# Start of a windowed-attention and gated-FFN kernel: first loads on other queues, an edge mask on ScalarE, a decode in PSUM, and 600 steps in a written order

## Chip, cores and metric

One core of one Trainium2 chip. The time is device microseconds (us) of one execution of the program. The kernel before took 701.21 us, the median of 3 runs (701.18, 701.21 and 704.1).

## What is computed

The inputs are `x` of shape (4, 4160, 192) and `weight_gen` of shape (4, 4160, 8, 7), and the float32 weights of a feed-forward stage: `w_in` (192 x 1024), `conv_w` (3 x 1024) and `w_out` (1024 x 192).

```python
# stage 1: every position is a softmax-weighted sum of itself and the 6 positions before it, per head
w = exp(weight_gen - max(weight_gen, -1)); w = w / (sum(w, -1) + 1e-9)
x_pad = concatenate([zeros((B, 6, D)), x], axis=1)
x = einsum('bshk,bskhg->bshg', w, x_pad windows of 7).reshape(B, S, D)
# stage 2: gated feed-forward with a 3-tap convolution along the sequence
h = maximum(x @ w_in, 0)
conv = sum over k of conv_w[k] * h shifted by k - 1
out = (h * 1/(1 + exp(-conv))) @ w_out
```

## The kernel before

**Tiles.** The 4 x 4160 positions are cut into 128 segments of 130, one per partition. A block is 4 rows of each segment, 512 positions in all, and there are 33 blocks. The text calls them block 0, 1, 2 and so on.

**Attention of a block** (`head`). `w` is a tile of softmax weights: w0 serves block 0, w1 blocks 1 and 2, w2 blocks 3 and 4, w3 blocks 5 and 6. `ring` holds rows of x. Seven products `ring * w` (`tap`, L299, 128x768 each) go into `px` (four) and `py` (three), on POOL ("G") or VectorE ("V") as `PLAN` says. For blocks 0 to 2 TensorE transposes and adds all seven pieces itself (L347). From block 3 on, two DMAs that add while they copy (`fold1` L322, `fold2` L325) and a POOL addition (`fold3` L332) leave one piece for TensorE to transpose. The result is split into a rounded part H (ScalarE, L367) and a remainder (VectorE, L371).

**Feed-forward of a block.** A unit is one 128-column slice of w_in: five matmuls into a PSUM bank z (`mm1` L385), relu, middle tap and tanh on ScalarE (L391, L395, L409), two side taps and the gate on VectorE (L402, L447). Eight units make a block. `mm2` (L468) then multiplies by w_out, one 128-position output tile at a time.

**Weights.** The float inputs are read as raw bits and decoded in five steps (`decode_steps`, L140 to L158), then w_in is split into a high part (ScalarE, L663) and a low part (VectorE, L668). w_in comes in five pieces (`CH`): "m" pieces hold its first 128 rows, "f" pieces the other 64 rows, folded, which SyncE's queue then spreads (L682). f0 and m0 are columns 0 to 255, f1 and m1 256 to 511, m2 512 to 1023. `r_cw` is the raw `conv_w`; it is decoded in SBUF in a corner of `h` (24 partitions).

**Softmax of a `w` tile** (`sm_ops`). Maximum, subtraction, exp (ScalarE), sum, epsilon, reciprocal, normalization (L271). For the first 6 rows of each batch, `zero` (L276) multiplies by a 0/1 tile `edge`, since those rows look back before the sequence starts.

**What sets the order.** Every step is a task with an engine, a duration and dependencies. A list planner (`greedy`, `place`) places all tasks by estimated arrival times (`w_in_t`, `x_t_`, `CH`) and the program issues them in that order; each engine works in its own issue order. Steps of class "VK" are VectorE steps that read or write SBUF only. Ahead of the first POOL step after a VK step, a pair of tiny writes, `tok` (L960 on VectorE, L961 on POOL), makes POOL wait until VectorE has got there. The loads at the start are issued in program order on SyncE's and ScalarE's queues.

## Time and profile before

| | value |
|---|---|
| profiled execution | 701.24 us |
| its span | 699.5 us (1.74 us lie around it) |
| median of 3 runs | 701.21 us |
| busy: PE / DVE / ACT / POOL | 97% / 94% / 85% / 81% of the span |
| granted TensorE clock, mean | 0.995 |

PE is TensorE, DVE is VectorE, ACT is ScalarE, SP is SyncE, PEld the weight loads of TensorE. Busy shares are averages over the whole span: the start, where the change lies, has to be read from windows and the timeline. In a wait, the name behind the arrow is what ended it.

### The profile page before, as it was taken

Reading aid. Unit: us, or ns where it says so; the run is one execution under the profiler, and the core shown is the slowest. Engines: PE = TensorE matmul, PEld = TensorE weight load, DVE = VectorE, ACT = ScalarE, POOL = GpSimd, SP = SyncE. Lnnn points to the kernel's source line nnn. Section 1 sums busy time; section 2 is a strip of 40 time slices with the busy share of each in tenths; the row PEclk is TensorE's granted clock in tenths of the full one; section 3 lists DMA queues with packets and bytes.
Section 4 is the critical chain, followed back from the end, with each engine's and each line's share of the span. In section 5 each row is a group of like instructions: output and inputs, shape, how many; then the busy total and the mean of one; then the engine's idle time right before and its main releaser. Section 6 shows DMA issues by size and latency. Waiting matters only on the chain.

```text
span 699.5 us, 11223 instructions
## 1 busy us (share of the span) xinstructions
PE 676.5 (97%) x3749; PEld 615.3 (88%) x3749; DVE 657.0 (94%) x1067; ACT 597.3 (85%) x1140; POOL 568.8 (81%) x453
## 2 busy tenths in 40 slices
PE   1799999999999999999999999999999999999998
PEld 1688889999999999999999999999999999999998
DVE  6899999999999999999999999999999999999991
ACT  2488888988989998989899898989999898888982
POOL 3898899989899997989798898979799897981111
PEclk9899999999999999999999999999999999999999
DMA  7746989999889988979989788988979798693211
GB/s 225 195 123 133 222 193 210 212 219 202 186 189 204 225 208 197 204 192 211 212 165 203 189 206 195 214 201 196 193 158 210 178 209 188 151 195 99 83 53 46
DMA packets 70789, 127.61 MB, mean 182 GB/s; under 512 B 5046, under 2 KB 42573, under 8 KB 70732
## 3 DMA queue, kind: packets, MB, share of 16 engines
q0 software_dynamic: 20160, 58.99, 47.9%
q1 hardware_dynamic: 50090, 67.51, 30.0%
q8 instruction: 30, 0.49, 0.3%
q10 hardware_dynamic: 482, 0.40, 0.2%
q14 instruction: 27, 0.22, 0.1%
HBM read 20.51 MB, written 12.78 MB: 48 GB/s over the span
## 4 chain that ended last, share of the span: by engine, by line
PE 90%; DVE 4%; POOL 2%; DMA 1%; ACT 1%; issue 1%; DVEq 0%; POOLq 0%
PE ops L468 46%; PE z L385 41%; PE tp L347 3%; DVE z L402 1%; DMA r_cw<-in_moe_conv_w_dram 1%; POOL px L299 1%; PE z L468 1%; DMA stage<-in_moe_w_in_dram 0%; ACT h L391 0%; DVE gx L447 0%; DVE g L447 0%; DVE scr L150 0%; POOL w L249 0%; DVE dps L153 0%; ACT z L395 0%
## 5 line engine op out<-in xcount | busy, mean ns | idle before, releaser
L402 DVE SCALAR_TENSOR_TENSOR z<-h,cw,z 128x512 f32<-128x512 f32 (+1 forms) x528 | 375.9, 742 | 8.5 <-ACT z L395 5.0
L385 PE MATMUL z<-H,wi 128*128 128x512 f32 x1056 | 300.4, 406 | 0.0
L468 PE MATMUL ops<-wo,g 128*128 128x192 f32 x1536 | 273.4, 328 | 0.0
L468 PEld LDWEIGHTS ops<-wo,g 128*128 128x128 f32 x1536 | 246.7, 190 | 0.0
L385 PEld LDWEIGHTS z<-H,wi 128*128 128x128 f32 x1056 | 196.5, 190 | 36.4 <-DVE H L371 0.3
L299 POOL TENSOR_TENSOR px<-ring,w 128x768 f32<-128x768 f32 (+2 forms) x146 | 226.0, 1661 | 1.2
L395 ACT ACTIVATE z<-h,cw 128x512 f32<-128x512 f32 (+1 forms) x264 | 180.0, 682 | 4.6
L409 ACT ACTIVATE z<-z 128x512 f32<-128x512 f32 (+1 forms) x264 | 152.0, 578 | 18.4 <-DVE z L402 14.1
L299 POOL TENSOR_TENSOR py<-ring,w 128x768 f32<-128x768 f32 (+2 forms) x108 | 164.8, 1862 | 2.2 <-DMA px<-py 2.2
L391 ACT ACTIVATE h<-z 128x512 f32<-128x512 f32 x264 | 156.0, 592 | 11.2 <-PE z L385 10.7
L447 DVE SCALAR_TENSOR_TENSOR g<-z,h 128x512 f32<-128x512 f32 (+1 forms) x198 | 130.7, 676 | 1.0
L481 POOL TENSOR_TENSOR o<-o 128x768 f32<-128x768 f32 x30 | 68.0, 2266 | 47.4 <-ACT o L475 30.0
L385 PE MATMUL z<-L,wi 128*128 128x512 f32 x264 | 103.6, 392 | 0.0
L468 PE MATMUL ops<-wos,gx 128*128 128x384 f32 x480 | 90.0, 309 | 0.0
L475 ACT ACTIVATE o<-ops 128x384 f32<-128x384 f32 (+1 forms) x128 | 61.8, 484 | 27.3 <-PE ops L468 26.6
L468 PEld LDWEIGHTS ops<-wos,gx 128*128 128x128 f32 x480 | 75.1, 189 | 4.9
L332 POOL TENSOR_TENSOR px<-px 128x512 f32<-128x512 f32 (+1 forms) x60 | 72.8, 1459 | 4.0 <-DMA px<-px 4.0
L385 PEld LDWEIGHTS z<-L,wi 128*128 128x128 f32 x264 | 49.9, 189 | 11.2
L367 ACT ACTIVATE H<-tp 64x256 fp32r<-64x256 f32 (+1 forms) x93 | 42.6, 458 | 9.0 <-PE tp L347 8.6
L325 POOL DMA_DIRECT2D px<-px x30 | 38.0, 1268 | 10.4 <-DMA px<-py 10.2
L322 POOL DMA_DIRECT2D px<-py x30 | 38.5, 1284 | 9.7 <-POOL py L299 9.7
L347 PE MATMUL tp<-ident,px 128*128 128x128 f32 x228 | 38.2, 284 | 5.5 <-POOL px L299 3.6
(80 smaller groups left out, 389.3 us busy)
## 6 DMA issues: line engine op xcount, KB each, us to landing
px<-py POOLq DMA_DIRECT2D x30, 1152.0 KB, 9.0
h<-h SPq DMA_DIRECT2D x128, 256.0 KB, 4.7
px<-px POOLq DMA_DIRECT2D x30, 768.0 KB, 6.9
ring<-in_x_dram SPq DMA_DIRECT2D x31, 384.0 KB, 5.8
out_dram<-o SPq DMA_DIRECT2D x31, 384.0 KB, 6.1
w<-in_weight_gen_dram SPq DMA_DIRECT2D x15, 224.0 KB, 4.7
r_out<-in_moe_w_out_dram SPq DMA_DIRECT2D x4, 384.0 KB, 5.5
wi<-scr SPq DMA_DIRECT2D x8, 128.0 KB, 6.1
```

The lines of the kernel that those rows point to most:

```text
L299: eng.tensor_tensor(out=dst[:, a:b, :].rearrange("p s (h g) -> p s h g", g=GRP), in0=ring[:, p:p + n, :].rearrange("p s (h g) -> p s h g", ...
L332: nc.gpsimd.tensor_tensor(out=dst.rearrange("p (s d) -> p s d", s=R), in0=a[:, :, lo:hi], in1=b[:, :, lo:hi], op=ALU.add)
L347: nc.tensor.matmul(o, lhsT=a, rhs=ident, is_transpose=True, start=(start and c == 0), stop=(stop and c == len(ops) - 1))
L385: nc.tensor.matmul(out=z, lhsT=w[:, fs], rhs=h_t[j, nm], start=(i == 0), stop=(i == len(terms) - 1))
L391: nc.scalar.activation(out=hrow(f, 2, R), in_=z_t[j, f], func=ACTF.Relu)
L395: nc.scalar.activation(out=z_t[j, f][:, :no * P], in_=hrow(f, cc, no), func=ACTF.Copy, scale=cw[:, NF + f:NF + f + 1])
L402: nc.vector.scalar_tensor_tensor(out=z, in0=hrow(f, cc + d, no), scalar=cw[:, k * NF + f:k * NF + f + 1], in1=z, op0=ALU.mult, op1=ALU.add,)
L409: nc.scalar.activation(out=z, in_=z, func=ACTF.Tanh, scale=0.5)
L447: nc.vector.scalar_tensor_tensor(out=g_of(j, f), in0=z_t[j, f][:, :no * P], scalar=1.0, in1=hrow(f, cc, no), op0=ALU.add, op1=ALU.mult)
L468: nc.tensor.matmul(out=ps[:, 0:m], lhsT=g, rhs=w, start=(n == 0), stop=(n == len(terms) - 1))
L475: nc.scalar.activation(out=o_t[j][:, 0:n, i, :], in_=ps[:, 0:n * D].rearrange("p (b d) -> p b d", b=n), func=ACTF.Copy, scale=0.5)
L481: eng.tensor_tensor(out=o[:, 0, a:b], in0=o[:, 0, a:b], in1=o[:, 1, a:b], op=ALU.add)
```

## The change

The tables and functions, cut to the core; the 600 numbers of `ORDER` are left out but for its first line.

```diff
-    ("a", "GVGGVGG"),
+    ("a", "GVGGGGG"),
...
-SMX = ("VV", "VV", "GG", "GG")
+SMX = ("VG", "VV", "GG", "GG")
...
+T_CW = 3.7
+T_X = (9.0, 12.8, 14.6)
+T_W = (4.2, 11.1, 20.1, 21.1)
...
-    ("f", 0, 256, 5.2, "VGP", "G"),
-    ("m", 0, 256, 8.7, "VVP", "G"),
-    ("f", 256, 512, 17.0, "GVP", "V"),
-    ("m", 256, 512, 16.0, "VVP", "G"),
-    ("m", 512, 1024, 18.0, "VVP", "V"),
+    ("f", 0, 256, 5.3, "VGP", "G"),
+    ("m", 0, 256, 10.1, "VVP", "G"),
+    ("f", 256, 512, 15.7, "GVP", "V"),
+    ("m", 256, 512, 16.8, "VVP", "G"),
+    ("m", 512, 1024, 19.1, "VVP", "V"),
+)
+ORDER = (
+    "38 40 4 5 47 6 41 39 7 9 49 50 8 10 11 129 42 48 51 52 131 53 130 43 133 132 54 58 44 60 61 59 45 136 137 139 "
...
-            nc.gpsimd.memset(ring[0:1, slot(r0):p, :], 0.0)
+            nc.vector.memset(ring[0:1, slot(r0):p, :], 0.0)
...
         def zero():
-            k = min(n, TAPS - s0)
-            t4 = w()[:, :k * HEADS, :].rearrange("p (s h) k -> p s h k", h=HEADS)
-            E_[1].tensor_tensor(
-                out=t4, in0=t4, in1=edge[:, s0:s0 + k, :].unsqueeze(2).to_broadcast([P, k, HEADS, TAPS]), op=ALU.mult
-            )
+            for r in range(min(n, TAPS - s0)):
+                t3 = w()[:, r * HEADS:(r + 1) * HEADS, 0:TAPS - s0 - r]
+                nc.scalar.activation(out=t3, in_=t3, func=ACTF.Copy, scale=mask[:, 0:1])
...
-        load_w(0, nc.scalar)
+        nc.gpsimd.dma_start(out=r_cw, in_=conv_w.bitcast(I32).rearrange("k (c p b) -> (k c) p b", p=P, b=2))
+        load_w(0, nc.scalar, nc.sync)
         load_in(nc.sync, *CH[0][:3])
-        load_x(-TAPS, 3)
-        load_in(nc.scalar, *CH[1][:3])
-        nc.scalar.dma_start(out=r_cw, in_=conv_w.bitcast(I32).rearrange("k (c p b) -> (k c) p b", p=P, b=2))
+        load_x(-TAPS, 3, nc.scalar)
+        load_in(nc.sync, *CH[1][:3])
...
-        c0 = dec(cw_raw.bitcast(I32), r_cw, temps[0][0:3 * NF, 0:P], temps[1][0:3 * NF, 0:P], arrive(8.9), [], "VVS")[0]
+        c0 = dec(cw_raw.bitcast(I32), r_cw, temps[0][0:3 * NF, 0:P], temps[1][0:3 * NF, 0:P], arrive(T_CW), [], "VVP", own=True)[0]
...
+        head_ = [int(a) for a in ORDER.split()]
+        taken = set(head_)
+        rest = [i for i in sorted(range(nt), key=lambda i: (best[i], pos[i])) if i not in taken]
         pend, nk = False, 0
-        for i in sorted(range(nt), key=lambda i: (best[i], pos[i])):
+        for i in head_ + rest:
```

Of x's first load, the main part and the 15-partition part go on ScalarE's queue, the 112-partition part stays on SyncE's. Of w0's load, the 112-partition part goes on SyncE's queue. m0 moves from ScalarE's queue to SyncE's, behind x's first load. `r_cw` goes on POOL's queue, first of all. The `edge` tile and what built it are gone; the mask multiplies run on ScalarE, one per row, between the sum and the normalization (four for w0, three for w1). `conv_w` is decoded in a z bank of PSUM. Block 0 has one product on VectorE instead of two, and w0's normalization is on POOL.

Lines of the changed kernel are 25 to 28 higher, so that before's L299 is L324, L158 is L183, L249 is L276, L271 is L298, L668 is L692, L332 is L357 and L960 is L988. Three places of the order follow, each before and then after.

**VectorE, from the maximum of w0 on.** `m` and `r` are the maximum or sum and the reciprocal of a softmax tile, `dps` the PSUM bank of the decodes, `scr` scratch. Before:

```order
L246 TENSOR_REDUCE m<-w 128x32
L147 TENSOR_SCALAR dps<-dps 128x256
L249 TENSOR_TENSOR w<-w,m 128x224
L150 TENSOR_SCALAR scr_111<-dps 128x256
L153 SCALAR_TENSOR_TENSOR dps<-dps,scr_111 128x256
L255 TENSOR_REDUCE m<-w 128x32
L158 ISA dps<-dps,scr_111 128x512
L261 TENSOR_SCALAR m<-m 128x32
L264 RECIPROCAL r<-m 128x32
L668 TENSOR_TENSOR scr_111<-dps,scr_111 128x256
L271 TENSOR_TENSOR w<-w,r 128x224
L147 TENSOR_SCALAR h<-h 24x128
```

After, from the epsilon on:

```order
L288 TENSOR_SCALAR m<-m 128x32
L172 TENSOR_SCALAR dps<-dps 128x256
L175 TENSOR_SCALAR scr_110<-dps 128x256
L291 RECIPROCAL r<-m 128x32
L988 MEMSET tok_102 128x1
L178 SCALAR_TENSOR_TENSOR z<-z,h 24x128
L178 SCALAR_TENSOR_TENSOR dps<-dps,scr_110 128x256
L183 ISA dps<-dps,scr_110 128x512
L324 TENSOR_TENSOR px<-ring,w 128x768
L183 ISA h<-z,h 24x256
L988 MEMSET tok_103 128x1
L692 TENSOR_TENSOR scr_110<-dps,scr_110 128x256
```

The reciprocal now releases POOL through the first `tok`, the product and the last step of the `conv_w` decode stand ahead of f0's low part, and no normalization of w0 is left here.

**POOL, from its first `tok` on.** `py` and `px` are the products. Before:

```order
L961 MEMSET tok_103 128x1
L299 TENSOR_TENSOR px<-ring,w 128x768
L961 MEMSET tok_104 128x1
L299 TENSOR_TENSOR px<-ring,w 128x768
L961 MEMSET tok_105 128x1
L299 TENSOR_TENSOR py<-ring,w 128x768
L961 MEMSET tok_106 128x1
L299 TENSOR_TENSOR py<-ring,w 128x768
L961 MEMSET tok_107 128x1
L299 TENSOR_TENSOR px<-ring,w 128x768
L249 TENSOR_TENSOR w<-w,m 128x448 x2
L299 TENSOR_TENSOR px<-ring,w 128x768 x2
```

After:

```order
L989 MEMSET tok_102 128x1
L298 TENSOR_TENSOR w<-w,r 128x224
L324 TENSOR_TENSOR px<-ring,w 128x768 x2
L989 MEMSET tok_103 128x1
L324 TENSOR_TENSOR py<-ring,w 128x768 x3
L324 TENSOR_TENSOR px<-ring,w 128x768
L989 MEMSET tok_104 128x1
L324 TENSOR_TENSOR px<-ring,w 128x768 x3
L276 TENSOR_TENSOR w<-w,m 128x448
L324 TENSOR_TENSOR py<-ring,w 128x768 x2
```

Block 0's products stand in two runs instead of five pieces; the third `tok`, behind the normalization of w1 on VectorE, now stands ahead of block 1, and the subtractions of w2 and w3 stand inside block 1.

**POOL, from block 4's `fold2` DMA to its `fold3`.** Before:

```order
L325 DMA px<-px 128x2x768
L299 TENSOR_TENSOR py<-ring,w 128x768 x2
L961 MEMSET tok_108 128x1
L299 TENSOR_TENSOR py<-ring,w 128x768
L322 DMA px<-py 128x3x768
L332 TENSOR_TENSOR px<-px 128x512
```

After:

```order
L350 DMA px<-px 128x2x768
L324 TENSOR_TENSOR px<-ring,w 128x768
L324 TENSOR_TENSOR px<-ring,w 128x384 x2
L347 DMA px<-py 128x3x768
L989 MEMSET tok_105 128x1
L276 TENSOR_TENSOR w<-w,m 128x448
L324 TENSOR_TENSOR py<-ring,w 128x768
L324 TENSOR_TENSOR px<-ring,w 128x768 x2
L357 TENSOR_TENSOR px<-px 128x512
```

Products of block 6 and a subtraction now stand between the two. From block 3's `fold1` DMA to block 4's `fold3` there are 18 products now and 14 before.

## Rows read from the trace of the kernel before

**Rows 1.** Windows: us, busy us of PE, PEld, DVE, ACT, POOL; clock, DMA, GB/s.

```profile
5.00:62.20 57.20, 43.39 (x250) 36.47 (x250) 51.66 (x113) 36.07 (x81) 45.07 (x37) 0.94 0.57 163
5.00:12.30 7.30, 0.00 (x0) 0.00 (x0) 4.91 (x18) 2.39 (x8) 0.00 (x0) 1.00 0.77 231
62.20:82.00 19.80, 18.73 (x101) 17.06 (x102) 19.53 (x31) 15.99 (x31) 17.33 (x19) 1.00 0.96 219
200.00:660.00 460.00, 460.00 (x2544) 420.18 (x2543) 446.66 (x704) 415.15 (x784) 389.90 (x301) 1.00 0.83 189
```

**Rows 2.** Timeline, first 29 us: start, us, engine, line, instruction [idle before, releaser].

```profile
4.97 0.39 DVE L246 TENSOR_REDUCE m<-w 128x32 f32<-128x224 f32 x1 [1.53 <-DMA w<-in_weight_gen_dram]
...
8.21 0.38 DVE L271 TENSOR_TENSOR w<-w,r 128x224 f32<-128x224 f32 x1
...
10.88 0.21 DVE L147 TENSOR_SCALAR h<-h 24x128 f32<-24x128 f32 x1 [2.29 <-ACT h L140]
11.02 0.37 DVE L276 TENSOR_TENSOR w<-w,edge 128x224 f32<-128x224 f32 x1
...
12.52 1.54 POOL L299 TENSOR_TENSOR px<-ring,w 128x768 f32<-128x768 f32 x1
...
13.02 1.18 DVE L158 CUSTOM_DVE_ANT_0 h<-h 24x256 uint16<-24x256 uint16 x1
...
16.30 0.95 DVE L299 TENSOR_TENSOR px<-ring,w 128x768 f32<-128x768 f32 x1
...
18.56 1.70 DVE L299 TENSOR_TENSOR py<-ring,w 128x768 f32<-128x768 f32 x1
...
21.99 0.67 DVE L276 TENSOR_TENSOR w<-w,edge 128x168 f32<-128x168 f32 x1
...
24.82 1.89 POOL L249 TENSOR_TENSOR w<-w,m 128x448 f32<-128x448 f32 x2
...
28.34 0.26 ACT L259 ACTIVATE m<-m 128x64 f32<-128x64 f32 x1
```

**Rows 3.** Chain of waits, first 40 us: start, us, what.

```profile
4.16 6.35 DMA r_cw<-in_moe_conv_w_dram
```

**Rows 4.** Timeline of SyncE's DMA queue.

```profile
2.73 2.36 SPq L181 DMA_DIRECT2D ring<-in_x_dram  x2
8.94 0.36 SPq L206 DMA_DIRECT2D w<-in_weight_gen_dram  x1
```

**Rows 5.** DMA issues, 0.8 to 16.5 us: KB each, us to landing.

```profile
ring<-in_x_dram SPq DMA_DIRECT2D x1, 588.0 KB, 7.6
...
stage<-in_moe_w_in_dram ACTq DMA_DIRECT2D x1, 256.0 KB, 7.0
...
w<-in_weight_gen_dram ACTq DMA_DIRECT2D x1, 24.5 KB, 2.9
```

**Rows 6.** Timeline, TensorE.

```profile
62.19 0.92 PE L468 MATMUL ops<-wo,gx 128*128 128x192 f32 x4
...
80.80 0.66 PE L347 MATMUL tp<-ident,px 128*128 128x128 f32 x4 [1.07 <-POOL px L332]
...
101.05 0.60 PE L347 MATMUL tp<-ident,px 128*128 128x128 f32 x4
```

**Rows 7.** Timeline, POOL.

```profile
57.97 1.41 POOL L322 DMA_DIRECT2D px<-py  x1 [0.32 <-POOL py L299]
58.94 6.51 POOL L299 TENSOR_TENSOR px<-ring,w 128x768 f32<-128x768 f32 x4
67.62 3.33 POOL L299 TENSOR_TENSOR py<-ring,w 128x384 f32<-128x384 f32 x4 [2.17 <-DMA px<-py]
...
87.07 1.22 POOL L325 DMA_DIRECT2D px<-px  x1 [1.61 <-DMA px<-py]
...
94.59 2.46 POOL L332 TENSOR_TENSOR px<-px 128x512 f32<-128x512 f32 x2
```

**Rows 8.** DMA issues, 70 to 76 us.

```profile
px<-py POOLq DMA_DIRECT2D x1, 1152.0 KB, 12.6
```

53 lines of the change are left out of this document (27 added, 26 removed), and 20 rows, old and new, of the table ORDER.

## Prediction

> **What bounds the kernel now.** I read the windows first, to see in which stretch time can be won at all; then the start of the timeline for what VectorE and POOL wait for; then the DMA issues, which say when data can be there; and last the few places where TensorE itself had to wait. From 200 to 660 us TensorE is busy all 460 us and its order hardly changes, so nothing is to be had there [rows 1]. What the change can win is how early that saturated stretch begins. From 5 us to 62.2 us, where TensorE's first output tile starts [rows 6], VectorE is busy 51.66 of 57.2 us [rows 1]: only 5.5 us of idle time, and 2.29 of them are one wait [rows 2]. After 62.2 us it is busy 19.53 of 19.8 us. So in the start VectorE sets the pace, and POOL waits for it: its first product starts at 12.52 us [rows 2], although the last large part of x landed at 2.73 + 7.6 = 10.3 us [rows 4, 5]. The reader should see why: w0's reciprocal is done when its normalization starts at 8.21 us, but the edge multiply runs only at 11.02, since the first step of the `conv_w` decode stands ahead of it and waits for a load issued at 4.16 that took 6.35 us [rows 2, 3].
>
> TensorE waits just once later, 1.07 us at 80.80 us for POOL's sum of block 3 [rows 6]. So the first output tile is my milestone: what it gains, the end gains, unless POOL makes a new hole behind it.
>
> **The loads.** Of x, the 588 KB part shared the engines with m0's 256 KB [rows 5]; m0 now stands behind it. At the 231 GB/s of that stretch [rows 1] 256 KB are 1.1 us, so x is complete at about 9.2 us. Ends: 10.3, if sharing cost nothing, and 8.0, if a second part of the same size goes, too. w0's last part is issued one issue earlier; with 0.36 us for an issue and 2.9 us to land [rows 4, 5] its maximum starts at about 4.5 instead of 4.97 us [rows 2]. The profile also shows SyncE's queue silent from 5.09 (2.73 + 2.36) to 8.94 us [rows 4]; its next loads now come earlier, and none is on the milestone's path except through VectorE. The Trainium skill, "Trainium Kernel Development and Optimization", Key Constraints, speaks against this part: loads issued from several engines run on the same DMA engines and interleave, and only the issue time is saved. By that rule x lands at 10.3 us as before; this is rival D below. Rows 4 show at least one issue that was late by 3.9 us, which the rule allows.
>
> **VectorE's ledger** (first maximum to milestone). Removed: w0's normalization 0.38, the two edge multiplies 0.37 and 0.67, one product 1.70, and in the `conv_w` decode the last step, 1.18, becomes about 0.3, between the 0.21 of another step on 24 partitions and the old 1.18 (I take the low end, since the operand now comes from PSUM, and the long row ends just after POOL's product does: 13.02 + 1.18 against 12.52 + 1.54) [rows 2]. That is 3.12 + 0.88 = 4.0 us. Start: 0.5 us earlier. The memset of x's halo, now on VectorE, and the vanished `edge` steps lie before 4.5 us, where VectorE waited 1.53 us for w0 anyway [rows 2]; without that cover the memset could cost as much.
>
> Waits: the 2.29 us go, if `conv_w` has landed by about 4 us. In their place come up to 1.54 us, when the remaining product and POOL's first product, released by the same landing, meet: the port rows say that one of the two stands still (a VectorE product takes 0.95 us when POOL waits, 1.70 when POOL runs [rows 2]). A further 0.5 us comes since exp of w0 now stands behind f0's first decode step on ScalarE, and 0.5 since m0's decode must wait for f0's low part, which now stands behind the product. That is 2.5 us of new waits for 2.3 old ones. Ends: none of the new waits, or two more port turns of 1.54. **Sum: 4.0 + 0.5 - 0.2 = 4.3 us** earlier; by the ends 6.8 and 1.2.
>
> On the port, the Trainium skill ("SBUF — State Buffer", Who interferes with whom) says that a VectorE instruction with two SBUF inputs and a GpSimd instruction that reads SBUF exclude each other for a whole instruction; the 1.70 us row agrees. It does not say who is next when POOL has a second product queued, as it has here.
>
> **ScalarE.** Seven small mask multiplies are new. No row has their shape; the nearest, 128x64, takes 0.26 us [rows 2], so four take 1.04 us and seven 1.8. Ends: 0.2 and 0.5 each. w0's four run between the sum and the normalization, while VectorE does epsilon, two decode steps and the reciprocal, so I cost them at nothing; with none of that as a cover they would delay POOL's normalization by their 1.04 us (2.0 at the upper end), of which x's landing hides 0.4. ScalarE is busy 36.07 of 57.2 us [rows 1].
>
> **POOL.** New: one product, 1.54 us, w0's normalization, about 0.5 (half of the 0.95 us of a 448-element step [rows 2]; ends 0.4 and 1.0), and the issue of `conv_w`, about 1 us, the gap from one fold DMA to the next product (57.97 to 58.94) [rows 7]; it lies before 2 us, in place of the memset. w0 is normalized at 4.5 + (8.21 - 4.97) + 0.5 for exp + 0.6 for `tok` and itself = 8.8 us, so x at 9.2 us decides. Six products and one port turn: 9.2 + 9.2 + 0.95 = 19.4 us. Then POOL waits by `tok` for w1's normalization on VectorE, at the latest 4.3 us before the old start of block 1 (24.82 + 1.89 = 26.7), 22.4; I take 22. From there to block 3's first fold are 20 products, two subtractions and a normalization of 0.95: 30.8 + 2.85 = 33.7, and some 0.9 us of waiting for w2's reciprocal, late in VectorE's new order: 56.6 us against 57.97 [rows 7]. POOL gains only 1.4 us where VectorE gains 4.3. This is what is late next. Block 3: from that fold to the sum's start it has one product fewer (1.6) and its wait of 2.17 becomes 1.2, so TensorE gets the sum 1.4 + 1.6 + 1.0 = 4.0 us before 80.80, at 76.8. TensorE now does one more unit first, five matmuls or 0.9 us at the mean of the steady stretch (460 us for 2544 [rows 1]): it arrives at 80.80 - 1.07 - 4.3 + 0.9 = 76.3. The old hole is half gone or more, which would add 0.5 to 1 us; I don't count it, for VectorE has only 0.27 us of slack in that stretch.
>
> Block 4: its sum started at 94.59 us [rows 7], its first half was ready about 1.7 us later, and TensorE took it at 101.05: 4.8 us of slack. One more output tile ahead of it on TensorE (16 matmuls, 2.9), POOL's 1.4, and the old waits of 2.17 and 1.61 [rows 7] if they go, add 8.1; four more products (6.51 us [rows 7]) and the gain itself (4.3) take 10.8. What is left is 2.1 us. No new hole, but close.
>
> **Forecast.** The profiled execution took 701.24 us, 699.5 of them span; the median of the runs, 701.21, is the same. 701.24 - 4.3 = 696.9: **697.0 us**, own range 695.0 to 698.6.
>
> **Rivals.**
>
> A. *VectorE starves at the port.* POOL has two, then four products in a row, and the remaining product and w1's subtraction each meet them. If POOL's next product goes ahead of the waiting VectorE, each lost turn costs 1.54 us: 698.5 after one, 700.1 after two. For it: long runs on POOL are new, before a `tok` stood between most products. Against: no row shows a waiting VectorE passed over. 0.17.
>
> B. *POOL's block 4 becomes the bound*: the old DMA waits (3.8 us) come back in the new order. Then 2.1 us of slack become a hole of 1.7: 698.7. For: the folds share the DMA engines, one took 12.6 us [rows 8]. 0.08.
>
> C. *Slower:* `conv_w` lands late. Its first step now heads ScalarE's queue, with f0's decode and exp of w0 behind it, and everything above hangs on exp. exp starts after it about 0.9 us (two steps), and the first product 3.5 us behind the landing. From a landing at about 5.7 us on, each us costs one, and at 10.0 nothing is left of the gain. The old landing was at 10.5 us, issued at 4.16; issued at 1 us, the same 6.35 us give 7.4, 698.7. The slowest transfer on POOL's queue took 12.6 us [rows 8]: a landing at 13.6 gives 704.8. Against: it is 24 KB, and small loads at the start took 2.9 us [rows 5]. 0.06 for slower by that.
>
> D. *The loads arrive no earlier*, the change doesn't do what it says: x at 10.3 us, first product 1.1 us later, 698.1. Against: 256 KB in front are now behind. 0.11.
>
> **How the numbers follow.** The main case has 0.58, A 0.17, B 0.08, C 0.06, D 0.11. Changes under 0.5%, 3.5 us, cannot be told from none: the bound is 697.7 us. Of the main case 0.48 lies below it, of the rivals 0.07 (several reach it when the hole at 80.80 goes, too): faster 0.55, same 0.39, slower 0.06. The range runs from 695.0, the old hole gone and half of the new waits missing (VectorE's end of 6.8 is capped by POOL's block 3 at some 6), to 700.4, two lost turns; it leaves out C and tails.
>
> **What would show it.** Right: the first POOL product at 8.5 to 10 us, the block 1 products from about 22, TensorE's first output tile at 57 to 59 us, no wait above 1 us on TensorE behind it, and VectorE's busy time to that tile down by about 4 us. Wrong: VectorE rows of 2.5 us and more at the start (A); TensorE waiting for POOL's sum at about 97 to 100 us (B); ScalarE's first decode step waiting for `conv_w` beyond 6 us (C); a first product at 10.5 or later (D).

## The result, and the profile after

| | before | after |
|---|---|---|
| median of the runs beside each other | 702.06 us (4 runs, 701.18 to 704.1) | 695.12 us (4 runs, 694.71 to 696.19) |
| ratio | | 0.9899, 95% interval 0.9872 to 0.9927 |
| profiled execution, its span | 701.24, 699.5 us | 696.19, 694.5 us |

The kernel became faster by 6.9 us. A second set of runs of the same changed kernel (e17 below) gave 0.9906 [0.9892, 0.9920], 6.6 us. The forecast was 4.2 us. The profiled pair is 5.05 us apart, because the profiled before is among the fastest of its runs and the profiled after the slowest of its four; step by step the traces are compared as that pair. One run of 771.11 us in e6 and one of 1158.66 us in e15, at a lower granted clock, are left out below.

The windows of the changed kernel, cut at the same milestones as [rows 1] (columns: window, its length, busy us of PE, PEld, DVE, ACT, POOL, granted clock, DMA share, GB/s):

```profile
5.00:55.90 50.90, 40.59 (x249) 34.30 (x250) 47.59 (x105) 35.36 (x84) 44.86 (x35) 1.00 0.57 179
5.00:12.30 7.30, 0.00 (x0) 0.00 (x0) 6.14 (x17) 2.79 (x10) 3.31 (x4) 1.00 1.04 322
55.90:75.70 19.80, 19.80 (x107) 17.72 (x107) 19.64 (x31) 17.27 (x33) 18.99 (x18) 1.00 0.94 213
200.00:660.00 460.00, 460.00 (x2548) 420.61 (x2547) 446.07 (x703) 415.26 (x785) 383.69 (x297) 1.00 0.80 187
```

Against [rows 1] the start is 6.3 us shorter, 57.20 to 50.90. VectorE's busy time in it fell by 4.07 us (51.66 to 47.59), and its idle time by 2.23 (5.54 to 3.31). From 200 to 660 us TensorE is busy all 460 us in both.

The timeline of the changed kernel's first 28 us (start, us, engine, line, instruction, in brackets the idle time before it and what ended it):

```profile
4.90 0.28 ACT L165 ACTIVATE z<-r_cw 24x128 f32<-24x128 f32 x1 [2.60 <-DMA r_cw<-in_moe_conv_w_dram]
...
5.42 0.36 DVE L273 TENSOR_REDUCE m<-w 128x32 f32<-128x224 f32 x1
...
7.52 1.00 ACT L303 ACTIVATE w<-w,mask 128x56 f32<-128x56 f32 x4 [0.25 <-DVE m L282]
...
9.01 0.57 POOL L298 TENSOR_TENSOR w<-w,r 128x224 f32<-128x224 f32 x1
...
9.66 3.75 POOL L324 TENSOR_TENSOR px<-ring,w 128x768 f32<-128x768 f32 x2
9.78 2.24 DVE L324 TENSOR_TENSOR px<-ring,w 128x768 f32<-128x768 f32 x1
...
11.94 0.27 DVE L183 CUSTOM_DVE_ANT_0 h<-z,h 24x256 uint16<-24x256 uint16 x1
...
21.67 4.55 POOL L324 TENSOR_TENSOR px<-ring,w 128x768 f32<-128x768 f32 x3
...
23.27 0.65 PE L372 MATMUL tp<-ident,px 128*128 128x128 f32 x4 [1.37 <-DVE dps L183]
...
23.68 1.17 PE L410 MATMUL z<-H,wi 128*128 128x512 f32 x4
```

`conv_w` is there at 4.9 us rather than 10.5, and the first product starts at 9.66 instead of 12.52 us. Block 1 starts at 21.67 and the first unit of the feed-forward at 23.68 us.

What the first unit met before, by TensorE's timeline in the kernel before:

```profile
24.91 0.66 PE L347 MATMUL tp<-ident,px 128*128 128x128 f32 x4 [1.29 <-POOL px L299]
...
28.27 1.12 PE L347 MATMUL tp<-ident,px 128*128 128x128 f32 x4 [2.26 <-POOL px L299]
29.03 2.06 PE L385 MATMUL z<-H,wi 128*128 128x512 f32 x4
...
34.70 0.39 PE L385 MATMUL z<-L,wi 128*128 128x512 f32 x1
```

The windows of the kernel before there:

```profile
28.00:34.00 6.00, 5.73 (x16) 4.52 (x17) 5.63 (x11) 3.49 (x8) 6.00 (x6) 0.50 1.01 313
...
29.00:40.00 11.00, 11.00 (x53) 9.10 (x52) 9.33 (x20) 8.01 (x17) 11.00 (x9) 0.77 0.76 252
```

The windows of the kernel after, one over the same time and one from its first unit on:

```profile
28.00:34.00 6.00, 5.76 (x35) 4.63 (x33) 6.00 (x15) 5.51 (x13) 6.00 (x5) 1.00 0.78 270
...
23.70:33.90 10.20, 9.96 (x57) 8.15 (x55) 9.96 (x22) 8.66 (x19) 10.20 (x8) 1.00 0.86 283
```

Before, TensorE waited 1.29 and 2.26 us for POOL, and from 28 to 34 us it had a granted clock of 0.50, 1.2 GHz. The 15 matmuls of the first three units took 29.03 to 35.09, 6.06 us; after, at 1.00, they took 3.69 (23.68 to 27.37, the end of the last line below). VectorE, which works on what these units deliver, idled 1.67 of 11.00 us behind the first unit before and 0.24 of 10.20 after (0.24 of 11.00, too).

```profile
26.97 0.40 PE L410 MATMUL z<-L,wi 128*128 128x512 f32 x1
```

TensorE's timeline after, at the first output tile and where it takes block 3's sum:

```profile
55.93 0.88 PE L493 MATMUL ops<-wo,gx 128*128 128x192 f32 x4
...
74.82 0.60 PE L372 MATMUL tp<-ident,px 128*128 128x128 f32 x4
```

POOL's second fold and sum of block 3 in the kernel before, beside the lines of [rows 7]:

```profile
70.89 1.20 POOL L325 DMA_DIRECT2D px<-px  x1
...
79.08 2.34 POOL L332 TENSOR_TENSOR px<-px 128x512 f32<-128x512 f32 x2
```

POOL's timeline after, with the three steps that form the sum:

```profile
54.87 1.31 POOL L347 DMA_DIRECT2D px<-py  x1 [0.31 <-POOL px L324]
...
64.04 1.22 POOL L350 DMA_DIRECT2D px<-px  x1 [0.44 <-POOL px L324]
...
72.59 2.50 POOL L357 TENSOR_TENSOR px<-px 128x512 f32<-128x512 f32 x2
```

The first output tile starts 6.26 us earlier than in [rows 6]. `fold1` of block 3 is 3.10 us earlier than in [rows 7], and the sum 6.49 (79.08 to 72.59), because `fold2` now goes out at 64.04 instead of 70.89: before, block 4's `py` products stood ahead of it, and they waited 2.17 us for `fold1` to land. TensorE takes the sum without a wait, 5.98 us earlier; the hole of 1.07 us is gone.

A new wait of TensorE comes behind it. The chain of waits of the kernel after, from 104 to 118 us (start, us, what):

```profile
104.88 10.07 DMA h<-h
...
115.03 0.61 ACT h L416
...
117.05 0.69 DVE g L472
117.75 0.04 issue
117.79 1.45 PE z L410 x5
```

The DMA issues after, from 99 to 106 us (count, KB each, median us to landing):

```profile
px<-py POOLq DMA_DIRECT2D x1, 1152.0 KB, 12.5
px<-px POOLq DMA_DIRECT2D x1, 768.0 KB, 6.8
```

A `fold2` and a `fold1` were issued 1.7 us apart (101.01 and 102.71). Beside them a copy of 256 KB, the rows of h that one block hands to the next, needed 10.07 us; relu, the gate and TensorE (1.23 us at 117.79) waited in turn. Whether this costs anything at the end is the question of e3.

On TensorE's side the sum closes. Its busy time fell from 676.5 to 674.3 us, 2.2 us, about the 2.37 that its first three units gained. Its idle time fell by the other 2.8 us. This is bookkeeping and not a price: e1 and e7 ask what the clock is worth by itself.

### The profile page after: what moved, and what is told of

Its sections match the earlier page's. It is cut to its first block, busy times and chain, and to the rows that moved or that the text cites. A ratio compares the mean times of both kernels' runs of the same rounds, so it can differ in the third digit from the quotient of the medians.

```text
span 694.5 us, 11226 instructions
## 1 busy us (share of the span) xinstructions
PE 674.3 (97%) x3749; PEld 612.6 (88%) x3749; DVE 654.7 (94%) x1061; ACT 598.5 (86%) x1147; POOL 570.7 (82%) x451
## 4 chain that ended last, share of the span: by engine, by line
PE 84%; POOL 11%; issue 2%; DMA 1%; ACT 1%; DVE 0%; POOLq 0%; ACTq 0%
PE ops L493 43%; PE z L410 38%; POOL px L324 5%; POOL py L324 4%; PE tp L372 3%; DMA h<-h 1%; PE z L493 1%; POOL w L298 0%; POOL w L276 0%; POOL px L350 0%; POOL px L347 0%; POOL px L357 0%; ACT h L416 0%; DVE z L427 0%; ACT z L420 0%
## 5 line engine op out<-in xcount | busy, mean ns | idle before, releaser
L324 POOL TENSOR_TENSOR px<-ring,w 128x768 f32<-128x768 f32 (+2 forms) x146 | 232.7, 1703 | 1.1
L324 POOL TENSOR_TENSOR py<-ring,w 128x768 f32<-128x768 f32 (+3 forms) x109 | 170.4, 1912 | 0.0
L357 POOL TENSOR_TENSOR px<-px 128x512 f32<-128x512 f32 (+1 forms) x60 | 72.8, 1460 | 3.8 <-DMA px<-px 3.8
L350 POOL DMA_DIRECT2D px<-px x30 | 40.0, 1335 | 11.5 <-DMA px<-py 11.1
L472 DVE SCALAR_TENSOR_TENSOR z<-z,h 128x512 f32<-128x512 f32 x60 | 41.7, 695 | 1.3 <-ACT z L434 0.2
```

Source lines behind the costliest of these rows:

```text
L324: eng.tensor_tensor(out=dst[:, a:b, :].rearrange("p s (h g) -> p s h g", g=GRP), in0=ring[:, p:p + n, :].rearrange("p s (h g) -> p s h g", ...
L357: nc.gpsimd.tensor_tensor(out=dst.rearrange("p (s d) -> p s d", s=R), in0=a[:, :, lo:hi], in1=b[:, :, lo:hi], op=ALU.add)
L472: nc.vector.scalar_tensor_tensor(out=g_of(j, f), in0=z_t[j, f][:, :no * P], scalar=1.0, in1=hrow(f, cc, no), op0=ALU.add, op1=ALU.mult)
```

## Experiments

Milestones of every run in us: POOL's first product, TensorE's first unit and first output tile, and when it takes block 3's sum (in brackets its wait there). The ratio is to the kernel before, timed beside it. What a part is worth in the kernel after is told against 0.9902, the mean of after and e17, times 702.5 us; the intervals make that uncertain by some 1.5 us. The milestones are of one execution each. In the two of the changed kernel, after and e17, they lie 0.2 us (product) to 1.4 us (unit) apart, so smaller differences say little.

| run | ratio [95%] | product | unit | tile | sum | span |
|---|---|---|---|---|---|---|
| before | | 12.52 | 29.03 | 62.19 | 80.80 [1.07] | 699.5 |
| after | 0.9899 [0.9872, 0.9927] | 9.66 | 23.68 | 55.93 | 74.82 | 694.5 |
| e1 | 1.0027 [1.0015, 1.0038] | 11.89 | 28.05 | 59.97 | 81.03 [3.53] | 701.0 |
| e4 | 0.9994 [0.9981, 1.0007] | 11.78 | 28.25 | 60.37 | 81.17 [3.29] | 701.3 |
| e5 | 0.9973 [0.9964, 0.9982] | 12.95 | 29.45 | 62.60 | 79.93 | 698.8 |
| e6 | 0.9957 [0.9944, 0.9971] | 11.69 | 27.84 | 60.98 | 78.35 | 697.9 |
| e7 | 0.9968 [0.9956, 0.9981] | 11.69 | 28.01 | 60.22 | 78.45 [0.73] | 698.8 |
| e2 | 0.9932 [0.9916, 0.9948] | 9.35 | 25.67 | 58.88 | 77.41 | 696.2 |
| e8 | 0.9952 [0.9939, 0.9965] | 9.19 | 23.21 | 55.57 | 76.90 [2.28] | 697.5 |
| e9 | 0.9976 [0.9966, 0.9987] | 9.28 | 26.60 | 59.17 | 78.05 | 698.6 |
| e15 | 0.9956 [0.9940, 0.9972] | 9.46 | 24.84 | 57.77 | 76.71 | 697.7 |
| e10 | 0.9914 [0.9899, 0.9929] | 10.37 | 23.24 | 55.67 | 74.58 | 693.7 |
| e11 | 0.9991 [0.9980, 1.0002] | 14.17 | 28.49 | 60.96 | 79.89 | 699.1 |
| e12 | 0.9913 [0.9897, 0.9930] | 9.69 | 23.29 | 55.77 | 74.64 | 694.8 |
| e3 | 0.9913 [0.9895, 0.9932] | 9.45 | 23.46 | 55.76 | 74.68 | 694.7 |
| e13 | 0.9909 [0.9891, 0.9928] | 9.02 | 23.85 | 56.36 | 75.27 | 694.9 |
| e14 | 0.9915 [0.9894, 0.9936] | 9.76 | 23.12 | 55.67 | 74.54 | 694.6 |
| e16 | 0.9952 [0.9937, 0.9967] | 8.89 | 25.30 | 58.54 | 78.80 | 697.5 |
| e17 | 0.9906 [0.9892, 0.9920] | 9.44 | 22.30 | 54.80 | 73.67 | 693.8 |
| e18 | 0.9935 [0.9922, 0.9949] | 9.86 | 23.77 | 58.88 | 77.79 | 697.3 |

### First set: is it the clock, the order, the folds or the load?

**e1: before, with dummy transposes on TensorE** (10 and 20, into a PSUM bank that nothing reads; e7 has them, too) ahead of the two pieces it waits for, so that its clock stays up.

```diff
+        k = {(0, 3): 10, (1, 0): 20}.get((q, i), 0) if not part else 0
...
+            for _ in range(k):
+                nc.tensor.matmul(banks["warm"][:, 0:P], lhsT=ident, rhs=ident, is_transpose=True, start=True, stop=True)
```

> The kernel before, with 10 and 20 extra transposes of the identity into an unused z bank at the two places where TensorE waits for POOL's products (23.6 and 26.0 us); their result is not used. Theory 'VectorE's removed work': TensorE's first units are covered by VectorE's work, so the end does not move: 0 +- 0.5 us against before. Theory 'half clock': the granted clock stays at 1.0 from 27 to 34 us, the first 15 matmuls of three units take 3.7 instead of 6.07 us, VectorE's idle time of 1.67 us between 29 and 40 us goes, and the end comes 1.4 to 2.4 us earlier. If the clock still falls, the run tells nothing of the price, only that such transposes do not hold it.

In the profiled execution the clock is 1.00 from 25 to 40 us and the first tile 2.22 us earlier. Of these, 0.98 us were there at the first unit already, and 0.63 at the first product, ahead of any transpose; so the clock's part is 1.2 to 1.6 us. The end is 1.9 us later, which neither theory allowed. Timeline of e1, POOL and TensorE:

```profile
67.86 3.33 POOL L299 TENSOR_TENSOR py<-ring,w 128x384 f32<-128x384 f32 x4 [3.02 <-DMA px<-py]
...
81.03 1.12 PE L353 MATMUL tp<-ident,px 128*128 128x128 f32 x4 [3.53 <-POOL px L332]
81.79 2.05 PE L391 MATMUL z<-H,wi 128*128 128x512 f32 x4
```

The window of e1 there:

```profile
80.00:85.00 5.00, 3.98 (x13) 3.36 (x14) 1.60 (x3) 1.28 (x3) 5.00 (x6) 0.66 1.04 211
```

TensorE arrives earlier at a sum that POOL delivers no earlier (79.24 us, before 79.08): the hole grows from 1.07 to 3.53 us, and the half clock comes back behind it. So in the kernel before, a gain at the first tile alone is worth nothing. As a price of the clock e1 is not clean: the mean clock of its 12 executions is 0.994 to 0.998, as in the kernel before.

**e2: after, without the written order.** The planner orders everything.

```diff
 ORDER = (
-    "38 40 4 5 47 6 41 39 7 9 49 50 ..."
+    ""
 )
```

> The changed kernel without the 600 written entries: the planner orders all steps, with the new loads, arrival times, mask and decode. Theory 'VectorE's removed work' (the parts carry the gain, the written order little): the removed work (edge multiplies, one product, the normalization, the decode's last step) is still gone, so at most 1 us is lost against the changed kernel, and it stays 4 us or more ahead of before. Theory 'order': what counts is when POOL's first product of block 1 ends (23.2 us) and that TensorE meets no half clock; the planner keeps the products in pieces behind VectorE's steps, and 2 us or more of the 5 are lost again.

The order is worth 0.0030 in the ratio, 2.1 us, though the intervals overlap; against the five variants that changed nothing (e3, e10, e12 to e14) it is 1.2 to 1.6. The other parts of the change keep 4.8. TensorE's holes without it are 1.52 us at 43.14 and 1.58 at 106.55, both for VectorE's remainder of an attention block.

**e3: after, with the two folds apart.** `fold1` of block 6 (647) stands just ahead of block 5's sum (551) and goes out at 106.53 instead of 102.71 us; `fold2` of block 6 (650) stands behind a product of block 7 (753).

```diff
-... 572 750 647 532 573 ... 564 566 551 591 ... 553 662 650 614 664 ... 610 753 554 555 ...
+... 572 750 532 573 ... 564 566 647 551 591 ... 553 662 614 664 ... 610 753 650 554 555 ...
```

> The changed kernel with two moves in the written order: block 6's first fold from right behind block 5's second fold to behind the two products that follow (about 4 us later), and block 6's second fold one product later. Theory 'given back by a late carry' (the 256 KB copy of h rows issued at 104.3 us took 10.1 us beside 768 and 1152 KB of folds issued 1.7 us apart, and ScalarE, VectorE and TensorE waited for it): the copy lands in under 8 us, TensorE's hole of 1.23 us at 117.8 us goes, and the end comes 0.8 to 1.3 us earlier than the changed kernel. Theory 'VectorE is full anyway': the hole comes back elsewhere within the next blocks, 0 +- 0.4 us.

The copies of h land in 3.5 us (median of three from 98 to 112 us) and the hole at 117.79 is gone, so the folds did cause it. The end stays: TensorE now waits 0.90 us at 171.88 and 0.29 at 204.53, where it waited for nothing. The hole had moved, and no loss by it is seen at the end. TensorE in e3:

```profile
171.88 1.20 PE L390 MATMUL z<-H,wi 128*128 128x512 f32 x4 [0.90 <-DVE gx L440]
```

**e4: before, with `conv_w` first on POOL's queue.**

```diff
+        nc.gpsimd.dma_start(out=r_cw, in_=conv_w.bitcast(I32).rearrange("k (c p b) -> (k c) p b", p=P, b=2))
         load_w(0, nc.scalar)
...
-        nc.scalar.dma_start(out=r_cw, in_=conv_w.bitcast(I32).rearrange("k (c p b) -> (k c) p b", p=P, b=2))
```

> The kernel before with one thing changed: the load of conv_w goes on POOL's queue, first of all. Order and work of the engines stay. Theory 'VectorE's removed work and waits' as predicted: its wait of 2.29 us for this load goes, the first product on POOL starts when x has landed (10.3 instead of 12.5 us), and the end comes about 1.5 to 2.3 us earlier. Theory 'POOL's block 1 and the half clock': the first unit may come earlier by about as much, but TensorE still idles before it, the granted clock still falls, and the gain is the same 1.5 to 2.3 us with the half clock in the trace; if the fall moves or vanishes with the earlier start, up to 4 us.

The tile is 1.82 us earlier and the end the same, with a hole of 3.29 us at the sum and a clock of 0.72 from 80 to 85 us. This is e1 reached by another way, and the gain of neither theory came.

### Second set: POOL's sum

**e5: before, with `fold2` of block 3 ahead of block 4's `py` products and the sum ahead of the products that follow.**

```diff
-        for i in sorted(range(nt), key=lambda i: (best[i], pos[i])):
+        seq = sorted(range(nt), key=lambda i: (best[i], pos[i]))
+        seq.remove(350)
+        seq.insert(seq.index(440), 350)
+        seq.remove(353)
+        seq.insert(seq.index(443), 353)
+        for i in seq:
```

> The kernel before with two moves in POOL's order and nothing else: block 3's second fold goes ahead of block 4's py products (67.6 instead of 70.9 us), and block 3's sum ahead of two products of blocks 4 and 5 (about 76.5 instead of 79.1 us). Theory 'POOL's sum of block 3 sets the end': TensorE's hole of 1.07 us at 80.8 goes and the end comes about 1.0 us earlier, not more, since TensorE itself gets there at 79.7 us. Theory 'VectorE sets the pace' (it has 0.27 us of slack from 62 to 82 us): 0.3 us at most.

The sum starts at 76.69 instead of 79.08 us and TensorE no longer waits for it. By the ratio that is 1.9 us, more than the hole of 1.07 that was to go; the two profiled spans are 0.7 apart, and where the rest comes from is not shown.

**e6: e5 and e4 together.** **e7: e6 and the dummy transposes of e1.** Their edits are those shown.

> The two moves and the early load of conv_w together, in the kernel before. Alone, the load brought TensorE's first output tile 1.8 us forward and the end nothing: the hole at block 3's sum grew from 1.07 to 3.29 us, and after it the granted clock was 0.5 for 3.4 us. Theory 'POOL's sum of block 3 sets the end': with the sum some 2.5 to 3 us earlier the hole shrinks to under 0.5 us, the half clock behind it is gone, and the end comes 2.5 to 3.2 us before that of the kernel before, though each part alone gives 0 and 1. Theory 'VectorE sets the pace': no more than the load alone gave and 0.3: 0 to 0.5 us.

> As the run before, with the extra transposes that hold the granted clock at 1.0 from 27 to 34 us. TensorE's first output tile comes at about 58.2 us (62.2 - 1.8 - 2.2). Theory 'POOL's sum sets the end': the sum is ready at about 78 us as in the run before and TensorE now waits some 2 us for it, so the end is within 0.6 us of the run before: the half clock at the start is covered by POOL. Theory 'half clock': 1.4 to 2.2 us earlier than the run before.

With the sum out of the way, `conv_w`, worth nothing alone (e4), is worth 0.0016 or 1.1 us more than e5, though the intervals overlap; the 3.0 us of both are what the theory of POOL's sum gave. The transposes add nothing. This is the cleaner test of the clock, since all five executions of e7 have 0.999 or 1.000 and the four of e6 0.998. e7 is 0.8 us slower (the intervals overlap): its sum is no earlier, and TensorE waits 0.73 us there and 1.45 at 91.71 for the gate.

**e8: after, with `fold2` of block 3 (350) issued late**, just ahead of block 4's `fold1` (444).

```diff
-... 324 346 350 325 310 ... 385 438 444 395 ...
+... 324 346 325 310 ... 385 438 350 444 395 ...
```

> The changed kernel with one DMA issue moved in the written order: block 3's second fold from right behind block 3's last product (64.0 us) to behind the three products of block 4 that follow (about 70 us, where the planner of before put it: behind block 4's products). Nothing is added. Theory 'POOL's sum of block 3 sets the end': the sum starts at about 77.5 instead of 72.6 us, TensorE waits about 4 us at 75 us, and with a half clock behind that hole the end comes 4 to 6 us later: nearly all of the change's gain goes, though VectorE's removed work is still gone. Theory 'VectorE's removed work': 1.5 us later at most.

`fold2` goes out at 69.19 us and POOL waits 3.94 us for its landing. TensorE, in e8:

```profile
76.90 0.66 PE L352 MATMUL tp<-ident,px 128*128 128x128 f32 x4 [2.28 <-POOL px L337]
```

The place of one DMA issue costs 0.0050 in the ratio, 3.5 us. The theory had 4 to 6: the hole is 2.28 us and not 4, and the clock stays at 1.00 behind it (75 to 95 us).

### Third set: what each part is worth, taken from the kernel after

**e9: the mask multiplies, w0's normalization and block 0's second product back on VectorE. e15: the same without the product.**

```diff
-    ("a", "GVGGGGG"),
+    ("a", "GVGGVGG"),
-SMX = ("VG", "VV", "GG", "GG")
+SMX = ("VV", "VV", "GG", "GG")
...
-            for r in range(min(n, TAPS - s0)):
...
-                nc.scalar.activation(out=t3, in_=t3, func=ACTF.Copy, scale=mask[:, 0:1])
...
+            E_[1].tensor_tensor(
+                out=t4, in0=t4, in1=edge[:, s0:s0 + k, :].unsqueeze(2).to_broadcast([P, k, HEADS, TAPS]), op=ALU.mult
+            )
```

The `edge` tile and the steps that build it come back, too.

> The changed kernel with VectorE's work of the start put back (the two edge multiplies in place of ScalarE's seven mask multiplies, w0's normalization, a second product of block 0), the written order, the loads and the decode in PSUM kept: 0.37 + 0.67 + 0.38 + 1.70 = 3.1 us more on VectorE, one product and a normalization (2.1 us) less on POOL. Theory 'VectorE's removed work': the end comes 3.1 us later, since VectorE is busy 47.6 of 50.7 us up to the first output tile. Theory 'POOL's sum of block 3': POOL waited 1.74 us for VectorE at 21.6 us anyway and has 2.1 us less to do, so what counts is how late w1's normalization gets: between 1 and 3 us later. Under 1 us would say that the moved work was worth little in itself and the order and loads were all.

> The changed kernel with the edge multiplies and w0's normalization back on VectorE (0.37 + 0.67 + 0.38 = 1.4 us there; 1.7 us less on ScalarE, 0.57 us less on POOL), but with one product of block 0 on VectorE as in the changed kernel. All three with the second product cost 4.1 us of span. Theory 'VectorE's work counts in full up to w1's normalization': 1.0 to 1.5 us of span. Theory 'the second product alone did it': under 0.5 us.

e9 gives back 5.2 us, e15 3.8. That is more than the work itself (3.1 and 1.4 us), and more than any of the theories allowed. In e15 the first unit meets what it met before the change, by TensorE's timeline:

```profile
24.22 0.97 PE L375 MATMUL tp<-ident,px 128*128 128x128 f32 x4 [2.50 <-DVE dps L184]
24.84 2.05 PE L413 MATMUL z<-H,wi 128*128 128x512 f32 x4
```

The window of e15 behind it has a granted clock of 0.72:

```profile
25.00:30.00 5.00, 5.00 (x19) 3.97 (x18) 4.18 (x8) 2.94 (x6) 5.00 (x5) 0.72 0.96 321
```

In e9 the same window has 0.66, behind a wait of 2.68 us. How the 3.8 and the 5.2 us divide between the work and the clock is not shown.

**e10: x, w0 and m0 loaded on the queues of before.** `conv_w` stays first.

```diff
-        load_w(0, nc.scalar, nc.sync)
+        load_w(0, nc.scalar)
-        load_x(-TAPS, 3, nc.scalar)
-        load_in(nc.sync, *CH[1][:3])
+        load_x(-TAPS, 3)
+        load_in(nc.scalar, *CH[1][:3])
```

> The changed kernel with the first loads on the queues of before (w0 on ScalarE's, x on SyncE's, w_in's second piece on ScalarE's), conv_w's load alone stays first on POOL's queue. Theory 'x lands about 1 us later': first product at 10.5 instead of 9.7 us, VectorE's product too, and the end 0.7 to 1.1 us later. Theory 'covered': POOL waits 1.74 us for VectorE at 21.6 us and VectorE 0.5 to 2 us for ScalarE before 13 us, so nothing is lost: 0 +- 0.4 us.

The first product starts 0.71 us later, having waited for x, and the end is the same within the intervals. Timeline of e10, where VectorE is first at the port it shares with POOL:

```profile
10.32 0.96 DVE L324 TENSOR_TENSOR px<-ring,w 128x768 f32<-128x768 f32 x1 [0.18 <-DMA ring<-in_x_dram]
10.37 3.82 POOL L324 TENSOR_TENSOR px<-ring,w 128x768 f32<-128x768 f32 x2 [0.50 <-DMA ring<-in_x_dram]
```

In after POOL was first by 0.12 us, and VectorE's product took 2.24 us instead of 0.96: in e10 it gains more at the port than it loses by x. The Trainium skill ("SBUF — State Buffer", Who interferes with whom) says whoever starts first keeps the shared port for its whole instruction; these rows agree.

The price of x alone is seen beside e17, the changed kernel with the port order of e10. Timeline of e17:

```profile
9.39 0.96 DVE L324 TENSOR_TENSOR px<-ring,w 128x768 f32<-128x768 f32 x1
...
9.44 3.82 POOL L324 TENSOR_TENSOR px<-ring,w 128x768 f32<-128x768 f32 x2 [0.34 <-DMA ring<-in_x_dram]
```

In e10 the product is 0.93 us later than there, and the unit, the tile and the sum are 0.94, 0.87 and 0.91 us later; yet the spans are the same, 693.7 and 693.8. So in these two executions x's 0.9 us reach the sum of block 3 in full and not the end. A part of e17's lead goes at 171.52 us, where TensorE waits 0.39 us for VectorE's gate and e10 waits for nothing.

**e11: `conv_w` last on ScalarE's queue.**

```diff
-        nc.gpsimd.dma_start(out=r_cw, in_=conv_w.bitcast(I32).rearrange("k (c p b) -> (k c) p b", p=P, b=2))
...
         load_in(nc.sync, *CH[1][:3])
+        nc.scalar.dma_start(out=r_cw, in_=conv_w.bitcast(I32).rearrange("k (c p b) -> (k c) p b", p=P, b=2))
```

> The changed kernel with conv_w's load as the last of ScalarE's first loads instead of POOL's first. Its first decode step stands at the head of ScalarE's queue, with f0's decode and exp of w0 behind it. By the rival of the prediction each us of landing after 5.7 us costs one: landing at 8 to 10.5 us gives 2.3 to 4.8 us more at the first product and at the end. If POOL's sum of block 3 decides with slack left, less than that: 1 to 3 us. No change would say that exp does not wait behind it.

ScalarE's first step, in e11:

```profile
9.79 0.27 ACT L165 ACTIVATE z<-r_cw 24x128 f32<-24x128 f32 x1 [7.48 <-DMA r_cw<-in_moe_conv_w_dram]
```

4.89 us later than in after, and the tile is 5.03 us later. The whole gain is gone (0.9991): 24 KB at the wrong place of a queue undo everything else. The load was issued at 4.74 instead of 1.36 us, so 3.4 of the 4.9 us are the time of issue. The cost is that of a late load in the new order, where w0's maximum on VectorE and exp on ScalarE stand behind this step: the maximum starts at 10.31 us in e11 and at 5.42 in after. In the kernel before it started at 4.97, though `conv_w` was there only at 10.5.

**e12: block 0 on POOL alone** (`"GVGGGGG"` becomes `"GGGGGGG"`).

> The changed kernel with block 0's last product on VectorE moved to POOL (VectorE's took 2.24 us beside POOL's product at 9.8 us). Theory 'VectorE's removed work': the end comes about 2 us earlier than the changed kernel. Theory 'POOL's sum of block 3': POOL has one product (1.5 us) more, the 1.74 us that it waits for VectorE at 21.6 us go, so its row comes no earlier and the end stays within 0.7 us, with a hole of 1 to 2 us on TensorE at block 3's sum or before the first unit.

Nothing. The turn at the port that the product no longer costs is paid by the next VectorE instruction with two SBUF inputs: w1's subtraction takes 1.81 us, in after 0.75.

### Fourth set: is there more?

**e13: w1's last softmax steps and block 1's first product earlier in the order. e14: e13 and e3. e18: e13 and e12, with the decode and units reordered as well. e16: e2 with e5's two moves. e17: after, once more.** The edit of e13:

```diff
-... 16 17 69 70 68 71 72 55 73 74 75 95 18 143 19 78 80 20 156 145 ...
+... 16 17 18 69 70 19 68 71 20 156 72 55 73 74 75 95 143 78 80 145 ...
```

> The changed kernel with four entries of the written order moved: epsilon, reciprocal and normalization of w1 and block 1's first product go ahead of the steps of the f1 decode that stand between them. No work is added or removed. In the changed kernel POOL waits 1.74 us at 21.6 us for that normalization, though VectorE could have done it some 2 us earlier. Theory 'POOL's start of block 1': POOL starts block 1 at about 19.9 instead of 21.7 us, TensorE's wait of 1.4 us before its first unit shrinks to under 0.7, block 3's sum is ready 1 to 1.8 us earlier, and the end comes 0.5 to 1.5 us before that of the changed kernel. Theory 'VectorE's total work': it is the same work, so 0 +- 0.4 us.

> As the run before, and with the folds of blocks 5 and 6 apart as in the third run. Theory 'POOL's start of block 1, then the late carry': with the start 1 us earlier the hole of 1.2 us at about 117 us is the next bound, and taking it away gives 0.5 to 1 us more than the run before. Theory 'VectorE is full from 57 us on': no more than the run before, since the hole comes back later, as it did in the third run.

> The changed kernel without the written order but with the two moves of POOL's order from the fifth run (block 3's second fold ahead of block 4's py products, its sum ahead of two products). Without the moves the planner's order gave a span of 696.2 us, 1.7 more than the written one. There TensorE took the sum at 77.4 us without a wait. Theory 'POOL's sum': what the written order is worth is this place, and the run comes within 0.5 us of the changed kernel. Theory 'first unit': TensorE starts its first unit at 25.7 instead of 23.7 us in the planner's order, its wait is elsewhere, and the moves change nothing: 0 +- 0.5 us against the planner's order.

> The changed kernel once more, unchanged. Five variants of it that moved nothing by more than 1 us (e3, e10, e12, e13, e14) had ratios of 0.9909 to 0.9915 to the kernel before, while the changed kernel itself had 0.9899 from four runs. If those variants cost nothing, this run gives 0.990 to 0.992; if each of them really cost 1 us, it gives 0.9885 to 0.9905.

> The changed kernel with all three things that stood in a row before TensorE's first unit taken away together, each of which alone gave nothing: block 0's last product moved from VectorE to POOL (VectorE does 2.2 us less), w1's normalization ahead of the f1 decode (POOL starts block 1 as soon as block 0 is done), and block 0's split into high part and remainder ahead of the m1 decode, with the second and third unit changing places. Theory 'a row of equal chains': only together do they give something, the first unit starts at 22.5 to 22.9 instead of 23.7 us and the end comes 0.5 to 1.5 us before that of the changed kernel. Theory 'VectorE and TensorE are full behind it': the first unit starts earlier, but the lead is used up by waits of TensorE for VectorE before 60 us, and the end is within 0.4 us.

e13 starts block 1 on POOL 1.83 us earlier, at 19.84, and the first unit is no earlier: it now waits for VectorE's split of block 0. Timeline of e13:

```profile
23.47 0.63 PE L352 MATMUL tp<-ident,px 128*128 128x128 f32 x4 [2.90 <-DVE L L376]
```

e14 is as e13: the hole at about 118 us is gone, and TensorE waits 0.91 us at 171.76 instead. The place is the same as in e3, e17 and, with 0.46 us at 172.52, e12: VectorE's gate some 172 us into the run is the next to hold TensorE in these four. In after and e10 it does not. e16 makes e2 slower by 0.0020 (1.4 us; the intervals overlap), against both theories, with a new hole of 1.44 us at 73.75 for VectorE's gate: the move that helped in e5 does not help in another order. e18 shortens POOL's, VectorE's and ScalarE's part together and loses 2 us against e17, timed beside it, where the theories had a gain or nothing: TensorE waits 1.75 us at 30.96 for w_in, and the window from 30 to 35 us has a clock of 0.66. e17 repeats the result, and its 0.9906 says that the five variants with 0.9909 to 0.9915 cost nothing; its port order was that of e10 (VectorE's product at 9.39, 0.96 us), and its first unit was at 22.30 us, 1.4 earlier than in the profiled after. No version was found that beats the changed kernel.

## Why the prediction was right and where it was wrong

The direction was right, the size too small: 4.2 us forecast, 6.9 measured, or 695.12 us where 697.0 were forecast. Of the 2.7 us, 0.85 are no step's fault: the forecast started from a median of 701.21, and beside the kernel after the kernel before had 702.06. The step that failed is the sum up to the first output tile: 4.3 us forecast, 6.26 measured. Its mis-sized term is VectorE's idle time, 0.3 us less forecast and 2.23 less measured. Behind the tile POOL's sum of block 3 was mis-sized, too: TensorE got it 5.98 us earlier, not 4.0. Step by step:

- **What bounds the kernel.** Right that the start decides: giving VectorE its work back costs 3.8 us (e15) or 5.2 (e9). Wrong in "what the first output tile gains, the end gains": in the kernel before, e1 and e4 win 2.2 and 1.8 us at that tile and nothing at the end, since POOL's sum of block 3 was as late as TensorE. Two chains end there at nearly the same time, and the 1.07 us of [rows 6] was the sign that POOL's was already the longer one. The tile itself came at 55.93 us, and 57 to 59 were forecast.
- **VectorE's removed work.** 4.0 us forecast, 4.07 measured. The rows that I had named are down by 4.03: the last `conv_w` step takes 0.27 us (0.3), and the others are gone. On ScalarE and POOL the four masks take 1.00 (1.04), the three 0.72, w0's normalization 0.57 (0.5). That the total agrees, too, is partly luck. The product that stays takes 2.24 us instead of 0.95, because its wait at the port stands inside its row, as busy time; I had put that turn among the waits. Against it, two side taps of 128x512 fewer are done ahead of the tile (7.0 us busy before, 5.9 after), which is work put off and not saved. In e17, where the product takes 0.96, VectorE is busy 46.52 us up to the tile, 5.14 less than before.
- **VectorE's idle time.** This step failed: 0.3 us less forecast (start 0.5 earlier, 0.2 more waits), 2.23 less measured. (With the turn at the port counted as a wait, as I had done, the waits fell by 0.94 and the work by 5.36, side taps included.) The start is 0.45 us later instead (5.42 against 4.97), since the `conv_w` step stands ahead of w0's maximum. Of the 2.23 us, 0.79 lie ahead of the first unit and 1.43 behind it (1.67 to 0.24), where the kernel before had TensorE at half clock. I had put this at nothing. The sign stood in the forecast's own first row: a granted clock of 0.94 over 57.20 us [rows 1] is 0.06 x 57.20 / 0.5 = 6.9 us at half clock. I read the busy times of that row and passed over its clock. This is the price at the tile; that it reaches the end is not shown, for holding the clock by itself brought nothing there (e7).
- **POOL.** Block 0's end and block 1's start (19.4 and 22 forecast; 19.84 and 21.67) were right. Block 3's first fold was forecast at 56.6 and came at 54.87: the 20 products took 1.50 us each from start to start, not the 1.54 that one is busy, which is 0.7 us, and the 0.9 us of waiting for w2's reciprocal did not come. The kernel before would have told: its same 20 products, two subtractions and a normalization took 33.15 us (24.82 to 57.97), and after they took 33.20. So POOL gained the 3.1 us of its earlier start in full, where I had 1.4. From that fold to the sum I counted 2.6 us less; it was 3.4, as the wait of 2.17 fell to 0.44 and not to 1.2. So the sum was 6 us earlier at TensorE, not 4.0, and the hole, of which I counted nothing, went entirely.
- **The new order.** I costed its places, but gave the order no price. It is worth 1.2 to 2.1 us (e2); one DMA in it 3.5 (e8).
- **The loads.** x was forecast at 9.2 us: in e17, where POOL waits for it, it is there at 9.44, in e10, with the old queues, at 10.37. So rival D did not occur. But my reason, m0's share of the engines, was at most a part of it. The last of x to land in e10 is a part of 78.8 KB, third on SyncE's queue: issued at 3.75 us, landed 6.5 us later. In e17 it is issued at 2.76 us on ScalarE's queue and takes 6.3. The large part is issued 0.2 us earlier (2.52 against 2.71) and takes 6.8 us instead of 7.1. So most of the 0.9 us is time of issue, and the rule of the Trainium skill ("Trainium Kernel Development and Optimization", Key Constraints) that only issue time is saved mostly holds here. For `conv_w` it mostly holds, too: of the 4.9 us that e11 loses at its landing 3.4 are time of issue, and each cost a microsecond at the tile. The step "x later by 1.1 us, the end 1.1 us later" failed: in e10 the end is the same.
- **Rivals.** A did not occur: the waiting VectorE product got the port after one product of POOL (9.78 + 2.24 = 12.02 us, with POOL's first of two ending at 11.2). B did not occur; block 4's sum was there without a wait. C had about the right price: 4.89 us later cost 5.03 us at the tile and left nothing of the gain (e11), though each us counts from 4.9 us on and not only from 5.7.
- **"No wait above 1 us on TensorE behind the first tile"** was wrong: 1.23 us at 117.79, for a copy that the two folds delayed. No cost of it is seen at the end (e3).

Shown: several chains of nearly equal length end together, and the gain needs them shortened together. Added to before alone, parts are worth 0 (`conv_w`), 1.9 (the sum) and -1.9 us (the clock alone), the first two together 3.0. Taken from after alone, they cost 6.2 (`conv_w`), 5.2 (VectorE's work), 3.5 (`fold2`) and some 2 us (the order), 17 in all of a gain of 7. Neither list adds up to it, and none of these numbers is "the" worth of a part.

Open is how the 6.9 us divide among the parts, and why executions of one kernel differ by 1.5 to 4 us. A part of that goes with the clock. In the kernel before, the 52 executions beside the experiments with a mean clock of 0.994 or 0.995 are 0.7 us slower than the 29 with 0.997 or 0.998, by their distance from the mean of their group. In e13 four executions at 1.000 average 695.8 us and two at 0.998 697.8; in e14 four at 0.999 or 1.000 average 695.9 and two at 0.998 698.9. Which is the cause and which the effect was not tested. The port order, which differs between the profiled after and e17, is another candidate, of 1.3 us, and was not tested by itself either.
